# Placing tokens between attention steps: ranks and lists read by ScalarE, other steps for ones, base and one store

## The chip, the cores and the metric

One core of a Trainium2 chip runs the whole program. The metric is device time in microseconds (us). TensorE (PE; its weight loads are PEld) multiplies, VectorE (DVE), ScalarE (ACT) and GpSimd (POOL) do the rest, SyncE (SP) issues most DMA transfers. Only TensorE, VectorE and ScalarE of this program touch PSUM.

## The reference

Attention for 8 batches of 8 heads, 576 tokens, 64 per head, with rotary positions on q and k; then a mixture of 8 experts (512 to 1024 to 512, ReLU) in which every token goes to the one expert of its largest gate logit.

```python
scores = scale * q_rot @ k_rot.T;  attn = exp(scores - max) / sum;  x = attn @ v      # (4608, 512)
e_idx = argmax(x @ w_gate);  gate_w = softmax(...)[e_idx];  eom = sigmoid(x @ w_output_gate)
for e in range(8):
    m = e_idx == e
    out[m] = gate_w[m] * eom[m, e] * (relu(x[m] @ w1[e]) @ w2[e])
```

## The kernel before, in words

**Attention.** Two heads make a pair; 32 pairs, four to a batch, run one after the other. A pair has nine units: 128 queries of one head against 576 keys, the last unit holding the 64 left-over queries of both heads. A unit goes through TensorE (scores, L491), VectorE (negative row maximum, "peak", L496), ScalarE (exponential, L505) and VectorE again (32 x 32 transposes, "turn", L511). Units go in groups: 0 and 1, 2 and 3, 4 alone, 5 and 6, 7 and 8. There are two score buffers in PSUM, so TensorE writes a unit's scores once the exponential of the unit two before it is done. The products with v (L533) lag behind by one pair; their PSUM tile `acc` is copied out by ScalarE (L540 to L542), turned back by TensorE ("back", L548) and divided by the sums on VectorE (L560, into `xb`). POOL prepares the next pairs: rotary products (L435, L439) and the low halves of k and q (L417), which wait for ScalarE's high halves (L409). It also adds to the sums (`rz`, L514), whose reciprocal VectorE takes (L517).

**The order** is written out by hand. A step is one unit; `Attention.at(g, k, f)` puts f at step g with rank k, and `step` runs rank 0 and 1, the turn of the unit before, then ranks 2 and 3. Each engine works through its instructions in the order in which they were issued. Within a step and rank, what was registered first comes first. `EVENTS` has the steps of a pair's own work, counted from the pair's first step: back (19, 1), division (19, 2), the rz add (10, 2), its reciprocal (12, 2), the casts of q's last rows to bd (1, 2), v loads 5 and 7.

**Placing** (`place`) runs once per batch, with its steps counted from 20 steps behind the start of the batch's last pair, so it is spread over the pairs that follow. Logits, the one-hot of the expert `oh`, running sums over the five chunks of 128 tokens (`ohs`), then: `base` (offset of each expert plus the count so far, POOL, step 15); `s14`, two TensorE matmuls that count the tokens before each token, into a free part of `acc`; `s14b` on VectorE, which adds base to these ranks and their total to `cnt`; products and sums of the ranks on POOL and VectorE; `ones(c)` (VectorE, L702) and `places(c)` (POOL, L709), the two operands of `s20` (TensorE, L717), which writes the token numbers to their places in a list of 288 columns in PSUM; `s21` (VectorE, L720) adds it to `lists`. With 36 steps to a batch, step 17 falls on step 1 of the fourth pair behind the batch's last one, steps 28 to 39 on the fifth and sixth, step 44 on step 1 of the seventh. `stores` send `xb` to HBM on SP's queue, in three pieces.

The last batch but one has its steps partly behind the end of attention, the last batch is placed during the expert stage. Behind the placing of the batch two before those, `table0` reads the lists on POOL (L914), and `fetch` starts four indirect gathers (L1013) for the first expert slots.

**Experts.** Slots of 256 or 128 tokens of one expert: tokens are gathered, transposed (L1043), split into high and low parts, multiplied (L1078, L1120), scaled and scattered. Weights come in pieces of 512 KB on SP's queue.

Of the kernel before, what the change touches and what calls it, by code (L numbers as in the profile page):

```python
# [15 lines left out]
ALU = mybir.AluOpType  # L16
# [3 lines left out]
S, H, D = 576, 8, 64  # L20
NP = H // 2
DM = H * D
E, FF = 8, 1024
P = 128
# [3 lines left out]
NCH = 5  # L28
# [29 lines left out]
PIECES = ((0, 4), (4, 8), (8, 13), (13, 18))  # L58
PLACE, PM = 20, 3
LISTED = 44  # L60
ROWS, PLACES = (28, 30, 32, 37, 39), (25, 29, 31, 34, 38)

TURN = 1

# [178 lines left out]
class Attention:  # L243


    def __init__(self, tc, nb, pools, cc, ident, ii, first, trib, oneb, cnt, zero, qk, v, xd, row, lists):
# [32 lines left out]
        for n, pr in enumerate(self.pairs):  # L279
            g, b = 9 * n, n // NP  # L280
            fs = {"kh": lambda pr=pr: pr.keyhi("A"), "kl": lambda pr=pr: pr.keylo("P"),
                  "qh": lambda pr=pr: pr.queryhi("A"), "ql": lambda pr=pr: pr.querylo("P"), "lasts": pr.lasts, "den0": pr.den0, "den1": pr.den1, "den2": pr.den2, "evict": pr.evict, "back": pr.back,
                  "newxb": lambda pr=pr, b=b: newxb(b) if pr.hp == 0 else None}
            fs["divide"] = lambda pr=pr, b=b: pr.divide(xbs[b])
            for t in range(2):
                fs[f"mult{t}"] = lambda pr=pr, t=t: pr.mult("P", t)
                fs[f"add{t}"] = lambda pr=pr, t=t: pr.add("P", t)
                fs[f"load{t}"] = lambda pr=pr, t=t: pr.load(t)
                fs[f"loadv{t}"] = lambda pr=pr, t=t: pr.loadv(t)
            for k, (b0, b1) in enumerate(PIECES):  # L290
                fs[f"av{k}"] = lambda pr=pr, b0=b0, b1=b1: [pr.values(j) for j in range(b0, b1)]
            early = dict(PREP.get(n, ()))
            for name, o, k in EVENTS:
                if n > 1 or name not in ("load1", "load0", "mult1", "add1", "kh", "kl", "mult0", "add0", "qh", "ql")[:10 if n == 0 else 2]:
                    at(g + early.get(name, o), k, fs[name])
            if n % NP == NP - 1:
                fs = place(tc, (px, px2, small), self.pairs, b, NT, cc, trib, oneb, cnt, xbs, xd, row, lists)
                if b == nb - 1:
                    self.last = fs
                else:  # L300
                    for k, p, f in fs:
                        at(g + PLACE + k, p, f)
# [57 lines left out]
class Pair:  # L360
# [190 lines left out]
    def flat(self):  # L551

        return self.acc.rearrange("p a b -> p (a b)")
# [16 lines left out]
def place(tc, pools, pairs, b, NT, cc, trib, oneb, cnt, xbs, xd, row, lists):  # L570

    nc = tc.nc
    p1, p2, small = pools

    last, ahead = b == NT // S - 1, b == NT // S - 2
    V = nc.vector if last else nc.gpsimd
    tt = V.tensor_tensor
    b3 = lambda t: t.unsqueeze(2).broadcast_to((P, NCH, E))
    T = {}

    def new(n, sh, dt=F32, **k):
        T[n] = p2.tile(sh, dt, tag=n, name=f"{n}{b}", **k)
        return T[n]
# [53 lines left out]
    def add(c):  # L637
        tt(out=T["ohs"][:, c + 1, :], in0=T["ohs"][:, c, :], in1=T["ohb"][:, c, :], op=ALU.add)

    def s10():  # L640
        V.tensor_scalar(T["eg"], T["eg"], 1.0, None, op0=ALU.add)

    def s11():
        tt(out=T["eg"], in0=T["eg"], in1=T["sm"], op=ALU.mult)

    def s12():
        nc.vector.reciprocal(T["eg"], T["eg"])

    def s13():

        V.tensor_copy(xbs[b][:, :, P], T["eg"])

    def store(i):
        r, n = b * S + i * 2 * P, 2 if i < 2 else 1
        if i < 2:
            nc.sync.dma_start(out=xd[r:r + 2 * P, :].rearrange("(c p) d -> p c d", p=P), in_=xbs[b][:, 2 * i:2 * i + 2, :])
        else:
            nc.sync.dma_start(out=xd[r:r + QR, :], in_=xbs[b][0:QR, 4, :])
# [10 lines left out]
    def s14():  # L669
# [3 lines left out]
        nc.tensor.matmul(flat(rk), oneb, flat(T["ohs"]), start=True, stop=False, skip_group_check=True)  # L673
        nc.tensor.matmul(flat(rk[:, 0:NCH, :]), trib, flat(T["ohb"]), start=False, stop=True, skip_group_check=True)

    def s14b():
        tt, rk = nc.vector.tensor_tensor, T["rk"]
        tt(out=new("pr", CE), in0=rk[:, 0:NCH, :], in1=T["base"].unsqueeze(1).broadcast_to((P, NCH, E)), op=ALU.add)
        tt(out=cnt, in0=rk[:, NCH, :], in1=cnt, op=ALU.add)

# [3 lines left out]
    def s16():  # L684
        nc.vector.tensor_reduce(new("po", [P, NCH]), T["pr"], axis=AX.X, op=ALU.add)
# [11 lines left out]
    def ones(c):  # L697

        if c == 0:
            new("ro", [P, NCH, lists.shape[1]], F32R, bufs=1)  # L700
            new("no", [P, NCH])
        nc.vector.tensor_scalar(T["ro"][:, c, :], row, T["hr"][:, c:c + 1], 0.0, op0=ALU.is_equal, op1=ALU.add,  # L702
                                accum_out=T["no"][:, c:c + 1])

    def places(c):

        if c == 0:
            new("pl", [P, NCH, P], F32R, bufs=1)
        V.tensor_scalar(T["pl"][:, c, :], row[:, 0:P], T["lo"][:, c:c + 1], T["tok"][:, c:c + 1], op0=ALU.is_equal,  # L709
                                op1=ALU.mult)  # L710
# [6 lines left out]
            nc.tensor.matmul(T["ls"], T["pl"][0:m, c, :], T["ro"][0:m, c, :], start=(c == 0), stop=(c == 4), skip_group_check=True)  # L717

    def s21():
        nc.vector.tensor_tensor(out=lists, in0=T["ls"], in1=lists, op=ALU.add)  # L720

    def both(f, c):
        return lambda: (f(), add(c))
# [1 line left out]
    no = lambda: None  # L725
    stores = lambda: [store(i) for i in range(3)]
    if last:
        run = lambda *fs: lambda: [f() for f in fs]
        return [s0, run(s1, s2), s3, run(s4, s5), run(s6, s7), run(s8, add0), both(s9, 1), lambda: [add(c) for c in (2, 3, 4)],
                run(s10, s11, s12), run(s13, base), no, no, no, no, s14, no, s14b, run(s15, s16, s17)] + [  # L730
                lambda c=c: (ones(c), places(c)) for c in range(NCH)] + [stores, no, s20, no, s21, no]

    def adds(*cs):
        return lambda: [add(c) for c in cs]

    fs = [(0, 2, s0), (2, 2, s1), (3, 2, s2), (5, 2, s3), (8, 2, s4), (9, 2, s5), (10, 2, s6), (11, 2, s7), (12, 2, add0),
          (12, 2, adds(1, 2)), (13, 2, adds(3, 4)), (15, 2, s8), (15, 2, base), (17, 1, s14), (17, 2, s14b), (18, 2, s9),
          (19, 2, lambda: (s10(), s11())), (20, 2, s15), (22, 2, lambda: (s16(), s12())), (23, 2, s17)]
    listed = LISTED - 9 if ahead else LISTED
    fs += [(listed, 1, s20), (listed, 2, s21)]  # L740
    fs += [(26 + c if ahead else ROWS[c], 3, lambda c=c: ones(c)) for c in range(NCH)]
    fs += [(26 + c if ahead else PLACES[c], 3, lambda c=c: places(c)) for c in range(NCH)]

    if b == NT // S - 2:
        fs += [(37, 2, lambda: (s13(), stores()))]
    else:
        fs += [(25, 2, s13), (31, 2, lambda: store(0)), (33, 2, lambda: store(1)), (34, 2, lambda: store(2)), (37, 2, no)]
    return fs


# [494 lines left out]
```

## Time and profile before

| what | value |
|---|---|
| time, median of 3 runs | 1031.89 us (1031.04 to 1037.81) |
| the profiled execution | 1033.53 us, its span 1031.7 us |
| granted TensorE clock, mean | 0.992 |
| busy: PE, DVE, ACT, POOL | 965.8, 813.4, 617.6, 596.1 us |
| VectorE's largest: peaks L496, turns L511, weight subtract L1037 | 206.1, 209.2, 252.9 us |
| VectorE's ones L702, list adds L720 | 40 of about 0.47 us, 8 of about 0.46 us |

Attention fills the first half of the span and the experts the second. Busy time of TensorE includes waiting of pipelined matmuls on each other, so a high share does not by itself make it the bound; the idle marks of the timeline, with what ended them, say more.

### The profile page before, as it was taken

The numbers are of one execution on the slowest core, as the hardware profiler recorded it, in microseconds if no ns is written. First come the engines' busy times: TensorE is split into PE (matmuls) and PEld (weight loads), VectorE is DVE, ScalarE is ACT, GpSimd is POOL, SyncE is SP. The second block draws the span as 40 slices with busy tenths as digits, with TensorE's granted clock in tenths as the row PEclk, the third lists the DMA queues.
The fourth block names the chain that finished last, engine by engine and source line by source line (L and its number), as shares of the span: only waits on it lengthen the run. The fifth ranks groups of instructions, "written<-read, shape, count | busy, mean of one in ns | idle before, by whom it ended". The sixth has DMA issues, their size and how long they took to land.

```text
span 1031.7 us, 34705 instructions
## 1 busy us (share of the span) xinstructions
PE 965.8 (94%) x14461; PEld 843.5 (82%) x14461; DVE 813.4 (79%) x1277; ACT 617.6 (60%) x1286; POOL 596.1 (58%) x605
## 2 busy tenths in 40 slices
PE   4999999999999999999799999999999999999995
PEld 4778877877777777777688899899898989899884
DVE  6889989988989888889668777667767876857772
ACT  4656666656656655666446455557666765857762
POOL 4777898897988978889630222126234443532621
PEclk9999999999999999999899999999999999999998
DMA  6655674665846748466539877758886977978960
GB/s 220 175 165 134 180 213 126 181 201 141 232 124 188 203 120 239 128 178 161 189 114 338 291 220 228 233 193 279 295 316 224 346 266 273 328 283 271 307 238 29
DMA packets 58209, 221.00 MB, mean 214 GB/s; under 512 B 9351, under 2 KB 9660, under 8 KB 53952
## 3 DMA queue, kind: packets, MB, share of 16 engines
q1 hardware_dynamic: 50304, 196.37, 61.0%
q0 software_dynamic: 6464, 21.26, 5.4%
q8 instruction: 115, 1.88, 0.8%
q10 hardware_dynamic: 1280, 1.11, 0.3%
q14 instruction: 46, 0.38, 0.1%
HBM read 198.64 MB, written 22.43 MB: 214 GB/s over the span
## 4 chain that ended last, share of the span: by engine, by line
PE 60%; POOL 15%; DVE 9%; issue 7%; ACT 6%; DMA 2%; POOLq 0%; ACTq 0%; DVEq 0%
PE py L1120 18%; PE ph L1078 14%; PE sc L491 11%; PE acc L533 7%; POOL raw L435 6%; PE ph L1070 4%; ACT pm L505 4%; DVE m L496 4%; PE acc L548 3%; POOL raw L439 2%; DVE wl L1037 2%; POOL kl L417 2%; POOL q L417 2%; PE mtp L1043 2%; DVE xb L560 1%
## 5 line engine op out<-in xcount | busy, mean ns | idle before, releaser
L505 ACT ACTIVATE pm<-sc,m 128x576 f32<-128x576 f32 x288 | 211.3, 738 | 201.0 <-DVE m L496 200.3
L1037 DVE TENSOR_TENSOR wl<-wr,wh 128x1024 fp32r<-128x1024 f32 x184 | 252.9, 1387 | 44.9 <-ACT wh L1035 42.8
L496 DVE TENSOR_REDUCE m<-sc 128x1 f32<-128x576 f32 x288 | 206.1, 750 | 54.0 <-PE sc L491 52.9
L491 PE MATMUL sc<-kh,q 64*128 64x288 f32 x1024 | 206.1, 325 | 20.5 <-ACT q L409 9.5
L533 PE MATMUL acc<-pt,v 32*64 32x128 f32 (+1 forms) x9216 | 198.2, 296 | 22.0 <-issue 13.9
L1120 PE MATMUL py<-wh,ht 128*128 128x512 f32 x640 | 214.5, 400 | 0.0
L1035 ACT CAST wh<-wr 128x1024 fp32r<-128x1024 f32 x208 | 212.6, 1050 | 0.0
L511 DVE STREAM_TRANSPOSE pt<-pm 128x576 f32<-128x576 f32 x288 | 209.2, 755 | 0.0
L491 PEld LDWEIGHTS sc<-kh,q 64*128 64x128 f32 x1024 | 153.4, 190 | 54.0 <-ACT pm L505 26.5
L533 PEld LDWEIGHTS acc<-pt,v 32*64 32x64 f32 x9216 | 158.9, 132 | 47.0 <-issue 33.0
L435 POOL TENSOR_TENSOR raw<-raw,rt 128x1152 f32<-128x1152 f32 x62 | 164.0, 2645 | 0.2
L1078 PE MATMUL ph<-xt,wh 128*128 128x256 f32 x896 | 160.9, 282 | 0.5 <-DVE xt L1059 0.5
L1078 PEld LDWEIGHTS ph<-xt,wh 128*128 128x128 f32 x896 | 138.3, 189 | 2.5 <-DVE xt L1059 1.5
L1120 PEld LDWEIGHTS py<-wh,ht 128*128 128x128 f32 x640 | 120.3, 188 | 24.2
L491 PE MATMUL sc<-kl,q 64*128 64x288 f32 x512 | 130.1, 308 | 0.0
L1078 PE MATMUL ph<-xt,wl 128*128 128x256 f32 x448 | 125.9, 281 | 0.0
L1120 PE MATMUL py<-wl,ht 128*128 128x512 f32 x320 | 125.0, 391 | 0.0
L1037 POOL TENSOR_TENSOR wl<-wr,wh 128x1024 fp32r<-128x1024 f32 x24 | 58.6, 2441 | 89.2 <-ACT wh L1035 83.2
L439 POOL TENSOR_TENSOR raw<-raw 128x576 f32<-128x576 f32 x62 | 87.7, 1414 | 1.9
L1094 ACT ACTIVATE ht<-ph 128x512 fp32r<-128x512 f32 x56 | 33.5, 598 | 90.1 <-PE ph L1078 90.1
L491 PEld LDWEIGHTS sc<-kl,q 64*128 64x128 f32 x512 | 86.3, 191 | 0.2 <-DVE kl L417 0.2
L1078 PEld LDWEIGHTS ph<-xt,wl 128*128 128x128 f32 x448 | 84.5, 189 | 0.1
(245 smaller groups left out, 1302.9 us busy)
## 6 DMA issues: line engine op xcount, KB each, us to landing
wr<-in_w SPq DMA_DIRECT2D x208, 512.0 KB, 5.2
raw<-in_qk SPq DMA_DIRECT2D x64, 576.0 KB, 4.8
v<-in_v SPq DMA_DIRECT2D x128, 288.0 KB, 5.9
xd<-xb SPq DMA_DIRECT2D x16, 640.0 KB, 6.8
xd<-xb SPq DMA_DIRECT2D x8, 160.0 KB, 5.0
rt<-in_rope ACTq DMA_DIRECT2D x1, 576.0 KB, 5.5
xg<-xd,2idx POOLq DMA_INDIRECT x18, 6.9
out<-y,2idx POOLq DMA_INDIRECT x18, 5.2
```

The source lines that it names most:

```text
L417: self.eng(eng).tensor_tensor(out=out, in0=a, in1=b, op=ALU.subtract)
L435: self.eng(eng).tensor_tensor(out=rv, in0=rv, in1=self.rt[:, 2 * t:2 * t + 2, x], op=ALU.mult)
L439: self.eng(eng).tensor_tensor(out=r[:, 2 * t, x], in0=r[:, 2 * t, x], in1=r[:, 2 * t + 1, x], op=ALU.add)
L491: self.nc.tensor.matmul(self.ps[i][:, a, :HS], st, mov[r, x], start=(n == 0), stop=(n == 2))
L496: nc.vector.tensor_reduce(self.m[i], ps[:, :, :HS], axis=AX.XY, op=ALU.max, negate=True)
L505: nc.scalar.activation(pe.rearrange("p (a b) -> p a b", a=2), self.ps[i][:, :, :HS], AF.Exp, bias=self.m[i], scale=1.0, accum_out=self.z[: ...
L511: self.nc.vector.transpose(out=self.pt[:, st[0] + 5 * st[1] if st else 4, :], in_=self.pc.pop(i))
L533: nc.tensor.matmul(self.acc[h * D:h * D + D, a, o:o + 32 * n], self.v[r, h, j, :], self.pt[r, u:u + n, 32 * j:32 * j + 32], start=(j == 0) ...
L1035: self.nc.scalar.copy(wh, r)
L1037: eng.tensor_tensor(out=wl, in0=r, in1=wh.bitcast(F32), op=ALU.subtract)
L1078: nc.tensor.matmul(ph[:, f, :], st[:, dc, fs], mv[:, dc, :], start=(n == 0), stop=(n == 11))
L1120: self.nc.tensor.matmul(py[h], st[:, f, hs], mv, start=(f == 0 and n == 0), stop=(f == 7 and n == 2))
```

## The change

Base is summed at step 6 instead of 15. The rank matmuls move from rank 1 to rank 2, behind the turning back of that step; a new `s14c` has ScalarE copy their result to SBUF, and `s14b` adds two steps later, on POOL instead of VectorE (on VectorE for the last batch, as before). The list products also move to rank 2; ScalarE copies their result (`lc`), and a new `s22` adds the copy to `lists`: three steps later on VectorE, or, for the batch whose lists `table0` reads, one step later on POOL. The ones move from steps 28, 30, 32, 37, 39 to 29, 29, 38, 38, 42 (last batch but one: from 26 to 30 to 29, 29, 29, 33, 33). The third store moves from step 34 to 40. The last batch's own order is unchanged.

```diff
-ROWS, PLACES = (28, 30, 32, 37, 39), (25, 29, 31, 34, 38)
+ROWS, AHEAD, PLACES = (29, 29, 38, 38, 42), (29, 29, 29, 33, 33), (25, 29, 31, 34, 38)
...
-    last, ahead = b == NT // S - 1, b == NT // S - 2
+    last, ahead, early = b == NT // S - 1, b == NT // S - 2, b == NT // S - 3
...
+    def s14c():
+        rc = new("rc", [P, NCH + 1, E])
+        nc.scalar.copy(rc, T["rk"])
+        T["rk"] = rc
+
     def s14b():
-        tt, rk = nc.vector.tensor_tensor, T["rk"]
+        rk = T["rk"]
...
     def s21():
-        nc.vector.tensor_tensor(out=lists, in0=T["ls"], in1=lists, op=ALU.add)
+        if last:
+            nc.vector.tensor_tensor(out=lists, in0=T["ls"], in1=lists, op=ALU.add)
+            return
+        nc.scalar.copy(new("lc", [P, lists.shape[1]], bufs=1), T["ls"])
+
+    def s22():
+        V = nc.gpsimd if early else nc.vector
+        V.tensor_tensor(out=lists, in0=T["lc"], in1=lists, op=ALU.add)
...
-          (12, 2, adds(1, 2)), (13, 2, adds(3, 4)), (15, 2, s8), (15, 2, base), (17, 1, s14), (17, 2, s14b), (18, 2, s9),
+          (12, 2, adds(1, 2)), (13, 2, adds(3, 4)), (6, 2, base), (15, 2, s8), (17, 2, s14), (17, 2, s14c), (19, 2, s14b), (18, 2, s9),
...
-    fs += [(listed, 1, s20), (listed, 2, s21)]
-    fs += [(26 + c if ahead else ROWS[c], 3, lambda c=c: ones(c)) for c in range(NCH)]
+    fs += [(listed, 2, s20), (listed, 2, s21), (listed + 1, 2, s22) if early else (listed + 3, 3, s22)]
+    fs += [((AHEAD if ahead else ROWS)[c], 3, lambda c=c: ones(c)) for c in range(NCH)]
...
-        fs += [(25, 2, s13), (31, 2, lambda: store(0)), (33, 2, lambda: store(1)), (34, 2, lambda: store(2)), (37, 2, no)]
+        fs += [(25, 2, s13), (31, 2, lambda: store(0)), (33, 2, lambda: store(1)), (40, 2, lambda: store(2)), (37, 2, no)]
```

## Rows read from the trace of the kernel before

**Rows 1.** The page: its first line, and one row of the DMA issues.
```profile
span 1031.7 us, 34705 instructions
...
xd<-xb SPq DMA_DIRECT2D x8, 160.0 KB, 5.0
```
**Rows 2.** Busy time by stretch: from:to, length, busy us (instructions) per engine, clock, DMA, GB/s.
```profile
540.00:560.00 20.00, 20.00 (x127) 17.84 (x126) 17.13 (x38) 13.06 (x18) 0.00 (x0) 1.00 0.93 345
```
**Rows 3.** Timeline, clean first group: start us, us, engine, instruction, [idle before <-releaser].
```profile
263.88 1.42 DVE L496 TENSOR_REDUCE m<-sc 128x1 f32<-128x576 f32 x2 [0.28 <-PE sc L491]
...
267.45 1.41 DVE L496 TENSOR_REDUCE m<-sc 128x1 f32<-128x576 f32 x2
```
**Rows 4.** Timeline, first group with the ranks.
```profile
248.18 1.42 DVE L496 TENSOR_REDUCE m<-sc 128x1 f32<-128x576 f32 x2 [0.19 <-PE sc L491]
...
251.54 0.20 DVE L678 TENSOR_TENSOR pr<-acc,base 128x40 f32<-128x40 f32 x1 [0.59 <-POOL base L661]
...
252.63 1.41 DVE L496 TENSOR_REDUCE m<-sc 128x1 f32<-128x576 f32 x2
```
**Rows 5.** Timeline, first group with the lists.
```profile
295.56 1.42 DVE L496 TENSOR_REDUCE m<-sc 128x1 f32<-128x576 f32 x2 [0.27 <-PE sc L491]
...
298.58 0.41 PE L491 MATMUL sc<-kh,q 64*128 64x288 f32 x2
...
298.69 0.46 DVE L720 TENSOR_TENSOR lists<-acc,lists 128x288 f32<-128x288 f32 x1 [0.36 <-PE acc L548]
...
299.34 0.40 PE L491 MATMUL sc<-kh,q 64*128 64x288 f32 x2
...
300.16 1.41 DVE L496 TENSOR_REDUCE m<-sc 128x1 f32<-128x576 f32 x2
```
**Rows 6.** Timeline, VectorE at steps 7 and 8, and at steps 3 to 5.
```profile
181.38 0.76 DVE L496 TENSOR_REDUCE m<-sc 128x1 f32<-128x576 f32 x1 [0.30 <-PE sc L491]
...
270.47 0.22 DVE L517 RECIPROCAL rz<-rz 128x10 f32<-128x10 f32 x1 [0.28 <-POOL rz L514]
...
270.61 0.45 DVE L702 TENSOR_SCALAR_CACHE_REDUCE ro<-row,hr 128x288 fp32r<-128x288 bf16 x1
...
270.98 0.75 DVE L496 TENSOR_REDUCE m<-sc 128x1 f32<-128x576 f32 x1
...
273.29 1.42 DVE L496 TENSOR_REDUCE m<-sc 128x1 f32<-128x576 f32 x2 [0.87 <-PE sc L491]
```
**Rows 7.** Groups of instructions, 60 to 500 us: xcount, busy us, mean ns, idle before.
```profile
L540 ACT COPY ac<-acc 128x512 f32<-128x512 f32 x28 | 16.3, 583 | 0.0
```
**Rows 8.** Waits, 60 to 500 us: in total us, times, longest.
```profile
POOL kl L417 <- ACT kh L409: 38.4, 20, 4.1
```
**Rows 9.** Timeline, the last pair of attention and the first expert transposes.
```profile
500.50 1.42 POOL L417 TENSOR_TENSOR q<-raw,q 128x576 fp32r<-128x576 f32 x1
...
510.28 0.20 DVE L678 TENSOR_TENSOR pr<-acc,base 128x40 f32<-128x40 f32 x1 [4.71 <-POOL base L661]
...
510.33 0.26 POOL L514 TENSOR_SCALAR rz<-z 128x10 f32<-128x10 f32 x1
...
515.77 0.76 DVE L496 TENSOR_REDUCE m<-sc 128x1 f32<-128x576 f32 x1 [1.55 <-PE sc L491]
...
524.11 0.66 PE L1043 MATMUL mtp<-ident,xg 128*128 128x128 f32 x4 [0.41 <-ACT pm L505]
```
**Rows 10.** Busy time by stretch, the last pair of attention.
```profile
512.00:516.00 4.00, 4.00 (x84) 3.29 (x76) 2.45 (x6) 1.65 (x5) 0.66 (x3) 0.50 1.02 418
516.00:520.00 4.00, 4.00 (x156) 3.58 (x140) 2.60 (x5) 1.56 (x4) 0.00 (x0) 0.89 0.07 17
```
**Rows 11.** Line L1037: duration ns min/median/max; then its timeline on VectorE and POOL.
```profile
L1037 DVE TENSOR_TENSOR wl<-wr,wh x184: 1201/1225/3449, 529.2 to 1012.9; 128x1024 fp32r<-128x1024 f32 x184
...
783.24 4.58 DVE L1037 TENSOR_TENSOR wl<-wr,wh 128x1024 fp32r<-128x1024 f32 x2
...
784.25 2.48 POOL L1037 TENSOR_TENSOR wl<-wr,wh 128x1024 fp32r<-128x1024 f32 x1 [0.69 <-issue]
```

## The prediction

> **What bounds the kernel now.** I read the page first, then the busy time by stretch, then the timeline of VectorE column group by column group. The span is 1031.7 us [rows 1]. From about 540 us on TensorE is busy without a gap [rows 2]: there it only matters when that stream starts. So the change is worth what it takes off the attention stage, up to about 523 us.
>
> In attention a pair of heads is nine units, worked on in groups: steps 0 and 1, 2 and 3, 4 alone, 5 and 6, 7 and 8. The distance between the first peak (L496) of one group and of the next is the clock of the stage. In a pair that carries no work of the placing, the first group takes 3.57 us, and the peak that ends it has no idle mark [rows 3]: VectorE sets the pace. With the ranks on it the group takes 4.45, of which 0.59 is VectorE waiting at L678 for POOL's base [rows 4]. With the lists it takes 4.60: TensorE does the five list products and only then the turning back, so L720 waits 0.36 for L548 and runs 0.46, and the division and the next peaks queue behind [rows 5]. Step 4 is the opposite: the peak after it stands 0.87 us idle, waiting for TensorE [rows 6].
>
> I name pairs by their distance from the last pair of a batch: +4 carries the ranks, +5 and +6 the ones, +7 the lists.
>
> **Ranks (+4).** Removed from VectorE ahead of the division: the wait for base and both adds. The group falls from 4.45 to the clean 3.57, 0.88 us. TensorE keeps its sum, only the order turns. ScalarE gains one copy of 48 columns; the trace has no such copy, the bounds are 0 and the 0.58 of the 512-column copy [rows 7]. I take 0.2, at no cost: it stands behind both exponentials of the group, and the next one waits for a VectorE peak. Queued behind it are only the two bd casts, needed at step 4. Six batches end inside the steady stage: 6 x 0.88 = **5.3 us**.
>
> POOL gets both adds, two small instructions of about 0.27 each, say 0.55. Where they stand, in +4, POOL has waited for ScalarE's kh (38.4 us in 20 waits over 440 us [rows 8]), but they come behind that wait, not in it. From there POOL runs on without a pause to the rz of +5, for which VectorE already waits 0.28 [rows 6]. So 0.55 per batch comes back as a longer wait at L517.
>
> **Lists (+7).** VectorE alone would give back 0.36 + 0.46 = 0.82. But TensorE does products and turning back in the same total, then the next scores, 298.58 to 299.74, and the peaks can start at 299.74 at the latest instead of 300.16 [rows 5]. Bounds 0.42 and 0.82; I take 0.49, near the lower, since TensorE is what comes next. Five batches (the sixth falls into the POOL-bound end below): **2.45 us**. ScalarE's copy of 288 columns, between 0 and 0.58 [rows 7], waits for the products; bd casts and then an exponential that waits for a peak are behind it. The later add of 0.46 goes into step 4's idle 0.87: nothing, unless the wait described under the rivals comes up.
>
> **Ones (+5, +6).** One costs VectorE 0.37 from its start to the next instruction's [rows 6]. Five leave steps 3, 5, 7, 3, 5: 1.85 us per batch if all are exposed. At steps 5 and 7 the peak behind would otherwise have waited 0.30 anyway [rows 6], so three of them give 0.07 to 0.2 each; the two at step 3 give all: together about 1.0 net of the one put at step 8 (0.05, again behind a 0.30 wait). Four go to step 4: 2 x 0.37 = 0.74 fits into 0.87. Less the 0.55 of POOL above: 0.45, bounds -0.9 and +1.3. Five batches: **2.25 us**. Base moved nine steps sooner is one POOL instruction of 0.2 moved past POOL's rotary work; nothing waits for it. The third store goes from ahead of a raw load to behind the first v load of the same pair on SP; the division that writes its buffer again stands four steps, about 7 us, behind, and 160 KB land in 5.0 [rows 1]: 0, and a few us per batch if SP were that late.
>
> **The end of attention.** In the last 50 us POOL itself is late: pair 31 starts right behind POOL's q, which ends at 501.92, and VectorE then stands 4.71 at L678, because base is queued behind four indirect gathers [rows 9]. Here pairs 28 to 30 go at POOL's pace, so nothing saved in them counts, and POOL's chain gets longer: the ranks' adds 0.55, base 0.2, the list add of this batch (576 columns take 1.42 [rows 9], so 288 about 0.75): **-1.6 us** on the start of pair 31.
>
> Then the gain: VectorE no longer stands at L678. Division and peaks of units 2 and 3 go at once, and the next stop is L517, which needs POOL's rz. That ended at 510.59, 8.7 us behind q; without base between them 8.4. So the peak of unit 4 comes 8.7 us behind q instead of 13.85 (515.77 - 501.92 [rows 9]): **5.2 us**. What is late next is POOL's gathers, and the wait shrinks to about 1.5 us. Behind the old stall TensorE's granted clock was 0.50 of full, the 1.2 GHz level, and 0.89 in the next stretch [rows 10], which is the one of unit 4: 4 us x 0.11, **0.45 us** that no longer go.
>
> Sum: 5.3 + 2.45 + 2.25 - 1.6 + 5.2 + 0.45 = 14.05, say 14.1 us. The expert stage keeps its length and starts sooner; its first transposes stood 22.2 us behind q [rows 9] and then come 16.5 behind it, and the gathers and weights had landed 14.1 us behind it (DMA share 1.02 to 516, 0.07 after [rows 10]): covered by 2 us.
>
> The profiled execution took 1033.5, 1.8 of it outside the span; 1033.5 - 14.1 = 1019.4. It stands 1.6 above the median of the runs shown, so **1018 us**.
>
> **Rivals.**
> The port. The old list add had one operand in PSUM; the new one reads both from SBUF. In the expert stage such a VectorE subtract takes 1.23 at the median and up to 3.45, and two of them took 4.58 where a POOL subtract of 2.48 had started in between: the second ran only when POOL was done [rows 11]. At step 4 of +7 POOL is on kl and q, about 1.42 each [rows 9]. If VectorE waits out one or both, the peak behind the add (1.42 or 2.84 + 0.46 - 0.87) is 1.0 to 2.4 us late per batch, five times: 1023 to 1030, say 1026. For: POOL is almost always busy there. Against: kl is nearly over when the add is due, and the idle 0.87 takes the rest.
> The Trainium skill, SBUF — State Buffer, Who interferes with whom, says a VectorE instruction with two SBUF inputs fully blocks against a GpSimd one that reads SBUF, whichever issues first keeping the port. The rows above agree; by that rule alone the sum would be the 1026 of this rival, and this case's attention trace does not show it for a list add.
>
> POOL everywhere. If POOL, not VectorE, sets the pace from +5 on in each batch, the ones give nothing: -2.25 and up to 1.6 more: 1020 to 1022. For: its wait at L517 is already there. Against: its kh waits show slack in the other pairs.
>
> The landing. If the first expert products wait for gathers or weights, what pair 31 gives is lost: 1018 + 5.65, about 1023.7. Against: the 2 us of cover.
>
> Slower: TensorE's clock. If the turned order of products, turning back and copies leaves TensorE standing once in each batch long enough for the clock to fall to 0.50 as behind the stall of pair 31, each fall costs 2.0 us (4 us at half the clock) beside a stall of the 1.5 us left in pair 31, 3.5 in all. From the fifth on the gain is gone; one in each of six batches makes 1018 + 21 = 1039. Only the one long stall shows in the rows [rows 10], and the change shortens it.
>
> The change not doing what it says: the wait for POOL moves from L678 to the reduce that reads the ranks, three groups later; POOL's adds and product end about 1.5 behind rz, over 3 us before that reduce. Price 0, no case of its own.
>
> **How the numbers follow.** Forecast 0.60 (1010 to 1022); port 0.11; POOL everywhere 0.10; landing 0.06; clock 0.04; more than forecast, stalls of TensorE that no rows explain going too, 0.09 (about 1009). The range 1008 to 1027 leaves out the clock, half of the port and a little at the lower end. About 1%, 10.3 us, is what a measurement can tell from no change: under 1021.6 is faster. That holds for 0.9 of the forecast, half of POOL everywhere and the case of more: 0.68; slower by over 1% half of the clock: 0.02; within 1% the rest, 0.30.
>
> **What would show it.** The ranks' group at 3.6, the lists' at 4.1, no idle mark left at either; the peak behind step 4 with almost no idle in +5 and +6; a wait at L517 of 0.6 to 0.9 in +5 and of 1 to 2 in pair 31; no clock under 0.9 at its end; the add of the lists at 0.4 to 0.5 (over 1 would be the port). I am wrong if pair 31 still stands 4 us, or if pairs without placing work get longer.

## The result

The changed kernel takes 1019.45 us at the median of four runs (1018.45 to 1020.77) against 1031.68 us before: ratio 0.9855, 95% interval 0.9826 to 0.9885; by the two medians alone the gain is 12.2 us. The forecast was 1018, in a range of 1008 to 1027. The profiled execution took 1019.95 against 1033.53, with a span of 1018.1 against 1031.7: 13.6 us less. The lines and pairs below are those of the prediction; line numbers behind L673 stand 5 to 12 higher than before.

The profile after is read in the same order as the one before: first the groups of VectorE in the steady pairs, then the last pair. Timeline of the changed kernel, the first group with the ranks (first three rows; the first and the last are its two first peaks), the one with the lists and the list add (next nine, with POOL beside the add), and the first pair with ones, from its second group on (last five):

```profile
246.13 1.42 DVE L496 TENSOR_REDUCE m<-sc 128x1 f32<-128x576 f32 x2 [0.19 <-PE sc L491]
...
248.82 0.95 DVE L560 TENSOR_TENSOR xb<-acc,rz 128x800 f32<-128x800 f32 x1
249.70 1.41 DVE L496 TENSOR_REDUCE m<-sc 128x1 f32<-128x576 f32 x2
...
292.50 1.42 DVE L496 TENSOR_REDUCE m<-sc 128x1 f32<-128x576 f32 x2
...
294.22 1.11 PE L722 MATMUL acc<-ro,pl 128*128 128x288 f32 x5
...
295.37 0.40 ACT L728 COPY lc<-acc 128x288 f32<-128x288 f32 x1 [0.47 <-PE acc L722]
...
295.80 0.99 DVE L560 TENSOR_TENSOR xb<-acc,rz 128x800 f32<-128x800 f32 x1 [0.36 <-ACT lc L728]
...
296.71 1.41 DVE L496 TENSOR_REDUCE m<-sc 128x1 f32<-128x576 f32 x2
...
299.75 1.41 POOL L417 TENSOR_TENSOR kl<-raw,kh 128x576 fp32r<-128x576 f32 x1 [2.15 <-ACT kh L409]
...
300.89 0.58 DVE L732 TENSOR_TENSOR lists<-lc,lists 128x288 f32<-128x288 f32 x1
...
301.12 0.47 POOL L619 TENSOR_TENSOR oh<-oh,ct 128x40 f32<-128x40 f32 x1
...
301.84 0.76 DVE L496 TENSOR_REDUCE m<-sc 128x1 f32<-128x576 f32 x1 [0.36 <-PE sc L491]
```
```profile
264.50 1.41 DVE L496 TENSOR_REDUCE m<-sc 128x1 f32<-128x576 f32 x2
...
267.93 0.22 DVE L517 RECIPROCAL rz<-rz 128x10 f32<-128x10 f32 x1 [0.69 <-POOL rz L514]
...
268.06 0.70 DVE L496 TENSOR_REDUCE m<-sc 128x1 f32<-128x576 f32 x1
...
269.77 0.51 DVE L707 TENSOR_SCALAR_CACHE_REDUCE ro<-row,hr 128x288 fp32r<-128x288 bf16 x1
...
270.32 1.42 DVE L496 TENSOR_REDUCE m<-sc 128x1 f32<-128x576 f32 x2
```

The ranks' group lasts 249.70 - 246.13 = 3.57 and has no idle mark inside, the clean value [rows 3, 4]. The lists' group lasts 4.21 instead of 4.60 [rows 5], and has a new mark: the division stands 0.36 for ScalarE's copy. Two ones fit at step 4: the peak behind them follows without a mark, 2.26 behind the peak of unit 4; it was 2.31 with 0.87 of them idle [rows 6]. The price is at L517, 0.69 of waiting instead of 0.28 [rows 6].

Timeline of the changed kernel, the last pair of attention and what follows:

```profile
491.33 1.40 POOL L417 TENSOR_TENSOR q<-raw,q 128x576 fp32r<-128x576 f32 x1
...
493.62 1.42 DVE L496 TENSOR_REDUCE m<-sc 128x1 f32<-128x576 f32 x2 [1.85 <-PE sc L491]
...
500.82 0.26 POOL L514 TENSOR_SCALAR rz<-z 128x10 f32<-128x10 f32 x1
501.12 0.22 DVE L517 RECIPROCAL rz<-rz 128x10 f32<-128x10 f32 x1 [1.18 <-POOL rz L514]
...
501.25 0.70 DVE L496 TENSOR_REDUCE m<-sc 128x1 f32<-128x576 f32 x1
...
509.27 0.66 PE L1055 MATMUL mtp<-ident,xg 128*128 128x128 f32 x4
...
519.00 1.88 PE L533 MATMUL acc<-pt,v 32*64 32x160 f32 x92 [2.04 <-issue]
...
520.81 0.51 PE L1090 MATMUL ph<-xt,wh 128*128 128x256 f32 x2
```

Busy time by stretch of the changed kernel (columns as in [rows 2]), the stretches that answer to [rows 10]:

```profile
500.00:504.00 4.00, 3.07 (x84) 2.44 (x88) 2.01 (x4) 1.02 (x3) 2.07 (x7) 1.00 1.02 412
504.00:508.00 4.00, 3.99 (x131) 3.31 (x132) 3.86 (x9) 2.12 (x5) 1.16 (x6) 1.00 0.50 203
```

The stall of 4.71 [rows 9] is gone. The next stop is POOL's rz, 1.18 us, and the peak of unit 4 comes 501.25 - 492.73 = 8.5 us behind POOL's q, where it came 13.85 behind it. The granted clock of this stretch is 1.00, the 2.4 GHz level, not 0.50.

By stretches, first peak to first peak, before and after: up to pair 4, 76.2 and 77.3 us; pairs 4 to 27, 379.0 and 367.5; pairs 28 to 30, 47.6 and 48.9; pair 31 to the first expert product (L1078, now L1090), 31.6 and 27.2; from there to the end, 497.3 in both. That is +1.1 - 11.5 + 1.3 - 4.4 = -13.5, or 13.6 without rounding. The other two profiled executions of the changed kernel (sets 2 and 3) give 8.3 and 10.2 in pairs 4 to 27 and 28.4 and 30.4 us from pair 31 to the first expert product, so one execution fixes these differences to 2 or 3 us and no better.

### The profile page after: what moved, and what is told of

Same layout as the page of the kernel before. It is cut to its first block, busy times and chain, and to the rows that moved or that the text cites. A ratio compares the mean times of both kernels' runs of the same rounds, so it can differ in the third digit from the quotient of the medians.

```text
span 1018.1 us, 34712 instructions
## 1 busy us (share of the span) xinstructions
PE 960.7 (94%) x14461; PEld 841.7 (83%) x14461; DVE 812.5 (80%) x1262; ACT 621.2 (61%) x1300; POOL 601.0 (59%) x620
## 4 chain that ended last, share of the span: by engine, by line
PE 70%; POOL 10%; DVE 8%; issue 6%; ACT 5%; DMA 1%; ACTq 0%; POOLq 0%; SPq 0%; DVEq 0%
PE py L1132 18%; PE sc L491 16%; PE ph L1090 15%; PE acc L533 10%; PE ph L1082 5%; POOL raw L435 4%; PE acc L548 4%; ACT pm L505 3%; DVE m L496 3%; DVE wl L1049 2%; POOL raw L439 2%; PE mtp L1055 2%; POOL q L417 1%; POOL pl L714 1%; ACT wh L1047 1%
## 5 line engine op out<-in xcount | busy, mean ns | idle before, releaser
L511 DVE STREAM_TRANSPOSE pt<-pm 128x576 f32<-128x576 f32 x288 | 207.1, 753 | 0.0
L1090 PE MATMUL ph<-xt,wh 128*128 128x256 f32 x896 | 160.9, 282 | 0.5 <-DVE xt L1071 0.5
L1090 PEld LDWEIGHTS ph<-xt,wh 128*128 128x128 f32 x896 | 138.2, 189 | 2.7 <-DVE xt L1071 1.5
L1090 PE MATMUL ph<-xt,wl 128*128 128x256 f32 x448 | 125.8, 281 | 0.0
L1090 PEld LDWEIGHTS ph<-xt,wl 128*128 128x128 f32 x448 | 84.5, 189 | 0.1
```

The source lines that it names most:

```text
L511: self.nc.vector.transpose(out=self.pt[:, st[0] + 5 * st[1] if st else 4, :], in_=self.pc.pop(i))
L1090: nc.tensor.matmul(ph[:, f, :], st[:, dc, fs], mv[:, dc, :], start=(n == 0), stop=(n == 11))
```

## The experiments

The three sets ran on three chips, where the kernel before took 1035.77, 1034.32 and 1034.89 us at the median. Ratios are to the kernel before on the same chip, and a gain in us is the ratio's, of that median; medians are set against each other within a set alone.

**Set 1: the parts alone, put into the kernel before.** Base alone:

```diff
-          (12, 2, adds(1, 2)), (13, 2, adds(3, 4)), (15, 2, s8), (15, 2, base), (17, 1, s14), (17, 2, s14b), (18, 2, s9),
+          (12, 2, adds(1, 2)), (13, 2, adds(3, 4)), (6, 2, base), (15, 2, s8), (17, 1, s14), (17, 2, s14b), (18, 2, s9),
```

> Only base moves, to step 6; all else as before. By my steps: the ranks' group loses its wait of 0.59 but keeps the adds on VectorE, 6 x 0.59 = 3.5 us; POOL's last chain gets 0.2 longer; pair 31 no longer stands 4.7 us at the rank add and stops at L517 instead, 5.3 + 0.45 us. Together -9.0: 1022.7 us. Rival (POOL is what holds pair 31, whatever waits for it): only the 3.5 comes, 1028.

Measured 1032.37, ratio 0.9959 (0.9936 to 0.9982): 4.2 us, under half of the 9. The ranks' pairs gave a little more than expected (15.70 to 15.00, 0.70 each and not 0.59), and the stall at L678 went. But pair 31 to the first expert product took 33.1 us, more than the 31.6 before. The busy time by stretch and TensorE's timeline of this kernel show where it went:

```profile
504.00:508.00 4.00, 3.74 (x52) 2.87 (x58) 1.18 (x3) 0.11 (x1) 0.74 (x4) 0.54 1.02 409
508.00:512.00 4.00, 4.00 (x103) 3.29 (x91) 1.34 (x3) 0.92 (x4) 0.00 (x0) 0.61 0.47 190
```
```profile
497.73 0.18 PE L673 MATMUL acc<-ohs,oneb 128*128 128x48 bf16 x1 [1.00 <-POOL ohs L638]
...
502.11 0.45 PE L533 MATMUL acc<-pt,v 32*64 32x160 f32 x4 [0.31 <-issue]
502.88 0.49 PE L533 MATMUL acc<-pt,v 32*64 32x160 f32 x4 [0.32 <-issue]
503.64 0.50 PE L533 MATMUL acc<-pt,v 32*64 32x128 f32 x4 [0.27 <-issue]
```

The rank matmuls, still ahead of the turning back, wait 1.00 for POOL's ohs, as they did before (0.98). Then TensorE does four products every 0.75 us while the DMA share is 1.02, and the clock is 0.54 and 0.61 for 8 us. The peak of unit 4 now stands 2.72 for TensorE. What makes TensorE so slow there was not found. So the expert transposes stand 20.1 behind the first peak of pair 31 instead of 21.3, and 2.7 more went between them and the first expert product, where the clock was 0.57 for 4 us.

The ranks whole, with `s14c` and `s14b` as in the change:

```diff
-          (12, 2, adds(1, 2)), (13, 2, adds(3, 4)), (15, 2, s8), (15, 2, base), (17, 1, s14), (17, 2, s14b), (18, 2, s9),
+          (12, 2, adds(1, 2)), (13, 2, adds(3, 4)), (6, 2, base), (15, 2, s8), (17, 2, s14), (17, 2, s14c), (19, 2, s14b), (18, 2, s9),
```

> Base at step 6, rank matmuls behind the turning back, ScalarE's copy, adds on POOL; lists, ones, store as before. By my steps: 6 x 0.88 = 5.3 from the ranks' group, less 5 x 0.55 at L517 of the pair behind, less 0.75 in POOL's last chain, and 5.75 from pair 31: -7.5, 1024 us, so no better than base alone. Rival (the adds on POOL cost nothing there): -11, 1020.5, clearly under base alone.

Measured 1027.62, ratio 0.9924 (0.9903 to 0.9945): 7.9 us, the total that was expected, but not by its terms. The ranks' pair is 14.81 long, and the six gave 5.4, as expected. Pair 31 to the first expert product takes 29.2, a gain of 2.4 and not 5.75. Pairs 4 to 27 are 8.7 shorter and not 2.55: L517 does wait longer in the pairs with ones (0.47 to 0.70), yet these ten pairs are 3.2 shorter, and TensorE's idle time in them that no releaser ends (stalls over 0.2 us, marked `issue`) fell from 4.8 to 0.7 us. That the total came out was luck.

The lists alone, with `s21` and `s22` as in the change, and behind it the ones alone:

```diff
-    fs += [(listed, 1, s20), (listed, 2, s21)]
+    fs += [(listed, 2, s20), (listed, 2, s21), (listed + 1, 2, s22) if early else (listed + 3, 3, s22)]
```

> Only the lists: products behind the turning back, ScalarE's copy, later add. By the lists' group after, 4.21 against 4.60, 5 x 0.39 = 2.0 us, less 0.8 for the add on POOL in its late stretch: -1.2, 1030.5 us. Rival (VectorE's port wait at step 4 eats it, or ScalarE's copy holds up more): 1032 or above.

```diff
-ROWS, PLACES = (28, 30, 32, 37, 39), (25, 29, 31, 34, 38)
+ROWS, AHEAD, PLACES = (29, 29, 38, 38, 42), (29, 29, 29, 33, 33), (25, 29, 31, 34, 38)
...
-    fs += [(26 + c if ahead else ROWS[c], 3, lambda c=c: ones(c)) for c in range(NCH)]
+    fs += [((AHEAD if ahead else ROWS)[c], 3, lambda c=c: ones(c)) for c in range(NCH)]
```

> Only the steps of the ones. By my steps 1.0 us per batch without the longer rz wait, and nothing in the last batch, which goes at POOL's pace: 5 x 1.0 = -5, 1027 us. Rival (POOL sets the pace from the pair of the ones on): under 1 us, 1031.

Lists: 1039.53, ratio 1.0032 (1.0012 to 1.0052). The lists' pair gained 0.34, near the 0.39 expected, but the ranks' pair grew by 0.22: its wait for base, late on POOL as before, took back what came sooner. Groups of instructions of this kernel, 60 to 490 us; the last figures are the idle time before the line and what ended it, which was 3.6 us before:

```profile
L678 DVE TENSOR_TENSOR pr<-acc,base 128x40 f32<-128x40 f32 x6 | 1.2, 200 | 4.7 <-POOL base L661 4.7
```

With pairs 28 to 30 0.9 longer, as expected, and pair 31 to the first expert product 1.0 longer, nothing is left, and the kernel is slower. Ones: 1035.5, ratio 0.9999 (0.9979 to 1.0020), against 5 us expected; in the trace pairs 4 to 27 are 2.4 us shorter, and the rest of the run hides it (the first four pairs, which the change does not touch, took 79.3 instead of 76.2). The sum of ranks, lists and ones over pairs 4 to 27 is -8.7 + 0.2 - 2.4 = -10.9, against -11.5, -8.3 and -10.2 in the three executions of the whole change: the parts add there within what single executions tell, though 3.2 of the 8.7 are the unexplained ones above. Over the whole run they don't: -7.9 + 3.3 - 0.1 = -4.7 by the ratios, against -12.6 below. Two reasons show in the traces: the lists alone pay nothing while base is late, and the stall of pair 31 stays with both of the smaller parts. That these make up the whole difference is not shown.

**Set 2: one edit each to the changed kernel.** The changed kernel itself, beside them:

> The changed kernel again, on the chip of these runs, to have it beside its parts and to see how far its executions lie apart. By its first timing 0.9855 of before, -15 us. The parts alone gave -8 (ranks), +3 (lists), 0 (ones), together -5. If the parts add up, -5 to -8 here; if, as their traces have it, they add up in the steady stretch (-11 of its own traces, pairs 4 to 28) and the rest is chance stalls of TensorE, -11 to -15.

Measured 1022.96, ratio 0.9878 (0.9839 to 0.9917): 12.6 us, the second of the two cases. That chance stalls are the rest is not shown by it. The division ahead of the copy of the lists:

```diff
-    fs += [(listed, 2, s20), (listed, 2, s21), (listed + 1, 2, s22) if early else (listed + 3, 3, s22)]
+    fs += [(listed, 2, s20), (listed, 3, s21), (listed + 1, 2, s22) if early else (listed + 3, 3, s22)]
```

> The changed kernel with ScalarE's copy of the lists one rank later, so that the division of that step is issued before it. In the changed kernel the division stands 0.36 at that copy. If it waits for the copy itself: the lists' group 4.21 to 3.85, 5 x 0.36, -1.8 us against the changed kernel. Rival (it waits for the list products, which end just before): no change, 0.

Measured 1022.36, ratio 0.9874 (0.9833 to 0.9915): 0.6 less at the median, which these runs can't tell from nothing. The trace can. Timeline of this kernel, the lists' group:

```profile
293.81 1.42 DVE L496 TENSOR_REDUCE m<-sc 128x1 f32<-128x576 f32 x2
...
296.69 0.99 DVE L560 TENSOR_TENSOR xb<-acc,rz 128x800 f32<-128x800 f32 x1
...
297.71 0.40 ACT L728 COPY lc<-acc 128x288 f32<-128x288 f32 x1 [1.01 <-DVE xb L560]
```

The division has no mark, and ScalarE's copy waits for the division instead. The group falls from 4.21 to 3.79, and the group behind it grows from 2.82 to 2.98, where TensorE, whose next products wait for the copy, is then late: 0.26 per pair net. So the 0.36 was the division's wait for the copy, and not TensorE.

The rank adds on VectorE at step 4, the product of the ranks one step later:

```diff
-        rk = T["rk"]
+        tt, rk = nc.vector.tensor_tensor, T["rk"]
...
-          (12, 2, adds(1, 2)), (13, 2, adds(3, 4)), (6, 2, base), (15, 2, s8), (17, 2, s14), (17, 2, s14c), (19, 2, s14b), (18, 2, s9),
-          (19, 2, lambda: (s10(), s11())), (20, 2, s15), (22, 2, lambda: (s16(), s12())), (23, 2, s17)]
+          (12, 2, adds(1, 2)), (13, 2, adds(3, 4)), (6, 2, base), (15, 2, s8), (17, 2, s14), (17, 2, s14c), (20, 3, s14b), (18, 2, s9),
+          (19, 2, lambda: (s10(), s11())), (21, 2, s15), (22, 2, lambda: (s16(), s12())), (23, 2, s17)]
```

> The changed kernel with the two rank adds on VectorE again, from ScalarE's copy, at step 20 behind the turn, where VectorE waits 0.87; the product on POOL one step later. If POOL's 0.55 for these adds is what lengthens the wait at L517 in the next pair: that wait from 0.45 to 0.70 down to 0 to 0.15, 5 x 0.5, and 0.55 off POOL's last chain: -3 us against the changed kernel. Rival (the adds, both operands in SBUF, wait for POOL's port): step 4 of the ranks' pair longer by 1 us or more, 0 to +3 us.

Measured 1036.14, ratio 1.0011 (0.9985 to 1.0037): the whole gain lost. My theory had the mechanism and missed its price. Groups of instructions of this kernel, 60 to 490 us, and a stretch of its timeline:

```profile
L517 DVE RECIPROCAL rz<-rz 128x10 f32<-128x10 f32 x27 | 4.7, 176 | 0.0
...
L690 DVE TENSOR_REDUCE po<-pr 128x5 f32<-128x40 f32 x6 | 1.2, 196 | 9.1 <-POOL pr L687 9.1
```
```profile
258.31 2.64 POOL L435 TENSOR_TENSOR raw<-raw,rt 128x1152 f32<-128x1152 f32 x1
...
260.92 0.27 POOL L687 TENSOR_TENSOR pr<-pr,oh 128x40 f32<-128x40 f32 x1
...
261.22 0.20 DVE L690 TENSOR_REDUCE po<-pr 128x5 f32<-128x40 f32 x1 [1.51 <-POOL pr L687]
```

L517 no longer waits in any pair (4.4 us over the same stretch in the changed kernel), as the theory says. But one step later the product stands on POOL behind q and behind the next pair's rotary product of 2.64 us, and L690 waits 1.51 for it in each of six batches: the ranks' pair is 16.17 long instead of 14.81, which is 8.2 of the 13 us. The pairs behind it are longer too, 3.5 in all, in an execution in which TensorE stood 4.0 in them without a releaser. This is the wait that moves to the reduce, which the prediction priced at nothing; in the changed kernel, with the product in its old place, the reduce has no mark.

The gathers three steps later:

```diff
-        att.at(g + 6, 2, moe.fetch)
+        att.at(g + 9, 2, moe.fetch)
```

> The changed kernel with the four gathers for the first expert slots three steps later, behind POOL's rz of pair 30. If pair 31 now stands only at rz: its wait of 1.18 at L517 goes, -1.2 us, no other place moves. Rival (the gathers then land too late, or POOL's rank adds behind them hold the ranks' reduce): +1 to +4 us.

Measured 1023.48, ratio 0.9884 (0.9848 to 0.9921): the same. L517 of pair 31 no longer waits, but the peak of unit 4 comes 7.39 us behind the first peak instead of 7.63. Timeline of this kernel, its last pair:

```profile
496.50 3.03 PE L548 MATMUL acc<-ii,ac 128*128 128x160 f32 x10
...
499.87 0.99 DVE L560 TENSOR_TENSOR xb<-acc,rz 128x800 f32<-128x800 f32 x1 [0.90 <-ACT rc L678]
```

Turning back took 3.03 here instead of 1.63, at a granted clock of 0.50, and the rank copy and the division behind it were late: 0.90 of the 1.18 went there. Pair 31 to the first expert product took 25.6 in this execution, the shortest of all, without the 2.04 stall of TensorE that the changed kernel had at its end.

**Set 3: the changed kernel again, and what the traces pointed to.**

> The changed kernel as it is, beside the next three on the same chip: they are measured against it. Its ratio to the kernel before was 0.9855 and 0.9878, so 0.984 to 0.989 again, 12 to 16 us.

```diff
-        fs += [(25, 2, s13), (31, 2, lambda: store(0)), (33, 2, lambda: store(1)), (40, 2, lambda: store(2)), (37, 2, no)]
+        fs += [(25, 2, s13), (31, 2, lambda: store(0)), (33, 2, lambda: store(1)), (34, 2, lambda: store(2)), (37, 2, no)]
```

> The changed kernel, with the third store back at step 34. My theory prices the move of the store at nothing: within 0.5 us of the changed kernel. The rival: a few us per batch if a transfer of SP's queue on one side or the other is waited for, so 5 us or more away from it, to either side.

The next has the edits of the division and of the gathers of set 2, both.

> The changed kernel with both single edits that showed in the trace: the copy of the lists behind the division (lists' pair 15.45 to 15.20, five times, 1.2 us) and the gathers three steps later (pair 31 to first expert product 27.2 or 28.4 to 25.6, 1.6 to 2.8 us). If they add, 3 to 4 us faster than the changed kernel. Rival: what the end gains is given back before the first expert product, as when base alone was moved; then 1 us.

The last has, beside these two:

```diff
-        rk = T["rk"]
+        tt, rk = nc.vector.tensor_tensor, T["rk"]
...
-          (12, 2, adds(1, 2)), (13, 2, adds(3, 4)), (6, 2, base), (15, 2, s8), (17, 2, s14), (17, 2, s14c), (19, 2, s14b), (18, 2, s9),
+          (12, 2, adds(1, 2)), (13, 2, adds(3, 4)), (6, 2, base), (15, 2, s8), (17, 2, s14), (17, 2, s14c), (20, 2, s14b), (18, 2, s9),
```

> The last one, and the rank adds on VectorE at step 4, but the product on POOL at its old step, so that it cannot fall behind POOL's q as it did when it went a step later. If the late product was the whole loss of that run: the wait at L690 is gone (it was 1.51), the waits at L517 in the pairs with ones fall from 0.7 to 0.2, the fourth pair stays at 14.8, and the kernel is about 2 us faster than the last one. Rival: POOL reaches the product before VectorE has added at step 4 and stands there, so the wait moves to POOL and to L690 or L517 again: the same as the last one, or up to 4 us slower.

| kernel | us, median | ratio to before, 95% |
|---|---|---|
| changed | 1023.45 | 0.9893 (0.9863 to 0.9922) |
| third store back at 34 | 1024.18 | 0.9899 (0.9870 to 0.9929) |
| division ahead of the copy, gathers later | 1021.35 | 0.9868 (0.9839 to 0.9897) |
| the same, rank adds on VectorE at step 4, product at its old step | 1024.41 | 0.9905 (0.9869 to 0.9941) |

The changed kernel came to 11.1 us, just under the 12 to 16 expected. The store: 0.7 us at the median, within the noise; pairs 4 to 27 take 368.5 and 368.8 us with it back and not; no sign of a wait, and a few us per batch are excluded. The two edits together: 2.1 us at the median, with intervals that overlap; the lists' pair is at 15.19, but pair 31 to the first expert product takes 30.7 against 30.4, so only the first edit shows, as the rival said. In all four profiled executions of this set the clock fell to 0.50 in pair 31, with the later gathers or without. It is the fastest kernel of its set, and not shown to beat the changed one. The last: groups of instructions of this kernel, 60 to 490 us:

```profile
L517 DVE RECIPROCAL rz<-rz 128x10 f32<-128x10 f32 x28 | 5.2, 186 | 2.2 <-POOL rz L514 2.0
...
L683 DVE TENSOR_TENSOR pr<-rc,base 128x40 f32<-128x40 f32 x6 | 1.9, 318 | 0.0
...
L690 DVE TENSOR_REDUCE po<-pr 128x5 f32<-128x40 f32 x6 | 0.9, 154 | 0.0
```

The wait at L690 is gone and the ranks' pair at 14.81, so the late product was the 8.2 us of that run; the wait at L517 is half of 4.4, and an undisturbed first pair with ones falls from 15.26 to 14.90. Yet the kernel is not faster: the 0.35 a batch is 2 us, and in the profiled executions TensorE's stalls that no releaser ends took 9.0 us here and 5.3 in the kernel without this edit (30 to 530 us, those over 0.2; last section). The rival's number came, without its mechanism: no wait moved to L690.

## Why the prediction was right

**The ranks** (5.3 forecast): exact. The six groups fell from 4.45 (two of them 4.47) to 3.57, 0.88 each; the six pairs by 5.4 in all. ScalarE's copy of 48 columns took 0.20, in front of nothing that was needed.

**The lists** (2.45): 0.39 each instead of 0.49, with 4.1 forecast and 4.21 measured, just under the lower bound of 0.42; five pairs gave 1.6, one of them with a stall of 0.3. The step that was off is "I take 0.49, near the lower, since TensorE is what comes next". TensorE was not next; ScalarE was. I asked what stands behind the copy on ScalarE and not who waits for it: the division reads the same `acc`, and stood 0.36 for the copy. The set 2 run took that wait away, and only then TensorE came, with 0.16.

**The ones** (2.25, or 0.45 a batch): where TensorE did not stall, the two pairs with ones went from 15.59 and 15.09 at the least to 15.26 and 14.86, 0.56 a batch. The ones alone, without POOL's added work, bring the groups with L517 from 3.53 to 3.18 and from 3.13 to 2.82; with the rank adds on POOL the first is back at 3.55. So POOL's adds cost VectorE 0.37 a batch against the 0.55 I gave them, and the waits at L517 (0.69 at first, 0.45 in others) are those forecast or a little less. All ten pairs together are 4.45 us shorter, 1.65 beyond five times 0.56, and TensorE's idle time in them that no releaser ends fell from 4.8 to 1.5 us. The other two executions of the changed kernel have 4.6 and 4.7 there, but a part of it is only moved: pair 25 stood 1.01 so before, and in seven of the eight later executions of the changed kernel and its variants pair 25 is free and pair 26, which carries lists, stands 0.9 to 1.9 instead. The first execution was spared that.

**The end of attention.** POOL's chain got 1.3 us longer instead of 1.6 (the three terms named for it add up to 1.5). The step "the peak of unit 4 comes 8.7 us behind q" measured 8.5, so 5.3 against 5.2, with L517 waiting 1.18 of the forecast 1 to 2. With the clock back at 1.00, the last group of the pair stands 5.9 closer to q (13.85 instead of 19.73), against 5.65 forecast for both terms. The expert transposes came 16.5 us behind q, as forecast, and no gather or weight was late. Then 1.2 us went: TensorE stood 2.04 at 519.00 ahead of the last products with v, where it had stood 1.03 before.

**What the sum left out.** Stalls of TensorE, early (pair 1 took 17.90 instead of 16.36) and at the end, took 2.3 us more than before; the steady pairs gave 11.5 instead of 10.0. These nearly cancel, so that the sum's 14.1 came within 0.5 of the 13.6 is in part luck. TensorE is not quite without a gap behind 540 us, as the prediction has it (18.91 of 20 us busy from 560 to 580 before), but that stage took 497.3 in both.

**The rivals.** The port: the list add took 0.58 beside POOL at step 4 and 0.45 at the end with POOL idle, so 0.13 and not the 1.0 to 2.4 of that rival. kl had 0.27 left when the add began, and POOL's next instruction was lengthened from 0.26 to 0.47. The Trainium skill, SBUF — State Buffer, Who interferes with whom, has a VectorE instruction with two SBUF inputs contend with a GpSimd one that reads SBUF, and the one that issues second fully blocked. Both were longer here, by 0.13 and 0.21, and the add by less than the 0.27 that kl had left; a longer meeting did not occur in attention. The clock: no fall once a batch (its mean over the first execution is 0.997), so that mechanism is refuted; in pair 31 the clock stayed at 1.00 in two of three profiled executions of the changed kernel and fell in the third:

Busy time by stretch, the changed kernel in set 3:

```profile
500.00:504.00 4.00, 3.40 (x19) 1.84 (x18) 1.33 (x3) 0.85 (x4) 2.97 (x8) 0.64 1.03 413
504.00:508.00 4.00, 4.00 (x74) 3.29 (x74) 1.44 (x2) 1.02 (x3) 0.00 (x0) 0.51 0.75 306
```

There pair 31 to the first expert product took 30.4 us and not 27.2: of the 5.65 of the two terms, some 3 hang on it. "No clock under 0.9 at its end" was right for the first execution and is not safe. The landing: refuted, as above. POOL everywhere: refuted in the steady pairs, where VectorE waits 24.9 us for TensorE's scores and 3.0 for POOL's rz (pairs 4 to 27), and where the ones gave 0.56 a batch though that wait grew.

## What to carry to other kernels

Work that must read PSUM in a crowded pair costs little as a copy on the engine that has just finished its part, with the arithmetic put where another engine waits; ask of such a copy not only what is queued behind it, but who waits for the tile that it reads. A small instruction may go a step later only if the large ones queued on that engine in between are shorter than its slack: one step cost 13 us here, 8.2 of it in the pairs of that instruction. What a part gains ahead of a late input is waited out at that input, so a part tried alone (the lists, with base still late) can measure as nothing and still belong to the gain.

## What the runs showed of the hardware that was not expected

Instructions arrive by DMA while the kernel runs, and some stalls of TensorE end shortly after a piece of them has landed. The page of the changed kernel lists that queue (queue, kind: packets, MB, share of 16 engines):

```profile
q8 instruction: 115, 1.88, 0.8%
```

The packets have 16,384 bytes each, and 14,461 matmuls and as many weight loads make about 250 TensorE instructions for each packet, and some 65 bytes for each instruction; that this queue is TensorE's is read from these figures and the times below. In the changed kernel a packet ran from 516.76 to 517.72 us, and the stall of 2.04 ended 1.28 us behind it. Its DMA queues from 516.5 to 517, and its busy time by stretch around it (PE columns 0.00 from 517 to 519, DMA share 0.96):

```profile
q8 instruction: 1, 0.02, 12.0%
```
```profile
516.00:517.00 1.00, 0.97 (x52) 0.67 (x39) 1.00 (x2) 0.00 (x0) 1.00 (x1) 1.00 1.08 393
517.00:519.00 2.00, 0.00 (x0) 0.00 (x0) 2.00 (x7) 0.19 (x1) 0.48 (x1) 1.00 0.96 236
```

In nine profiled executions, of the changed kernel (three) and of its six variants in sets 2 and 3, there are 48 stalls of TensorE over 0.35 us between 30 and 530 us that no semaphore explains; every one ended 1.20 to 1.59 us after such a packet. They cost 0.35 to 3.0 us each. The places come back: 28 of the 48 stand behind four of the 115 packets, the 4th (in every execution), the 34th, the 54th and the 70th. How long they are, and which of them occur, changes from execution to execution: 3.04 us behind the 4th packet, at 59 us, and 1.93 behind the 70th, at 429 us, in the set 2 execution of the changed kernel, 0.69 and none in the first. The kernel before and its parts in set 1 show 23 more, 1.21 to 1.87 us after a packet, and 18 that the profile marks alike and that have another cause: the products with v behind a division that the late base held up, 1.1 to 1.35 us in the ranks' pairs and 4.8 in pair 31. Runs of the changed kernel spread by 9 us in set 2 and by 5 in set 3, and stalls of this size are enough to hide gains of 1 to 2 us in the medians. That the late packet causes the stall is read from these times and was not tried; nor was what makes it late. The stutter of four products every 0.75 us in pair 31 has no packet at its steps, and its cause stays open.
